# Output projection of three segments in half-row, half-column matmuls

## The chip, the cores and the metric

The kernel runs on one core of a Trainium2 chip. The metric is the device time of one execution in microseconds (us). The core has a matmul engine (PE, with a weight-load side PEld), a vector engine (DVE), a scalar engine (ACT), a general engine (POOL) and a queue that issues most transfers (SP). Each takes its instructions in the order written and waits on semaphores of the others.

## The reference, cut to what matters

```python
h = _layernorm(x) * (1 + ca) + sa
x = x + ga * _A_ref(h, wq, wk, wv, wo, beta)      # attention, 4 segments of 512 rows
h = _layernorm(x) * (1 + cb) + sb
x = x + gb * _B_ref(h, w1, b1, w2, b2)            # squared-ReLU feed-forward
...
# the end of _A_ref: o holds the four segments' heads, 2048 x 512
o = (...)(jnp.stack(outs, 2).reshape(B, H, S, Dh), 0, 2, 1, 3).reshape(B, S, D)
return o @ wo
```

S is 2048, D is 512, 32 heads of 16, four segments of 512 rows. The change concerns `o @ wo` of the first three segments, 1536 rows.

## The kernel before, in words

A row tile is 128 of the 2048 rows, so there are 16, numbered `g`, four to a segment. A product in single precision is made of three matmuls on values split in a high and a low part (`F32R`): high by high, high by low, low by high. `KD` is 4: the inner dimension of 512 is four chunks `k` of 128 (`P`).

`wo_tile(g)` handles the output projection of one row tile. SP loads the tile's attention output `ot` (from `o_dram`) and its input rows `xw`; PE turns `ot` round (four transposes into a PSUM bank, `bwot`, L1259); ACT casts that to the high part of `oT` (L1267), DVE subtracts to get the low part (L1269). Then PE runs, for each chunk, the three matmuls of `wo_mm` (L1233 to L1235, 128 rows by 512 columns) into one PSUM bank, `bwop`. DVE adds `xw` to that bank (L1276) and takes the row's statistics (L603, L604). `WVO` holds `wo`, multiplied by the gate row and split in parts: four loads (L1223), four DVE products (L1224), four ACT casts (L1225), four DVE subtractions (L1226). There are two `oT` buffers and eight PSUM banks.

The tiles of the first three segments are done while the fourth segment's attention runs; the matmuls of both are mixed on PE. Attention works in a different array form: `qk` and `vproj` (L795, L865), the score matmuls `ba` and `bpb` (L903, L1072), and the transposes `bfin` (L1166) use 64 of the array's 128 rows each, in pairs, one for the upper and one for the lower half. The products with V, `bpv` (L1131), use 32 columns each. So PE has three modes, called F (all rows), R (half the rows), C (32 columns).

`qk` and `vproj` already work by halves of the rows: in turn 0 the upper half writes bank 0 and the lower half bank 1, in turn 1 the other way round, and between the turns stands a `fence`: ACT copies one element of an operand onto itself (L771), after the last matmul of turn 0 and ahead of the first of turn 1.

Every step is a node of a `Plan` with its engine, duration, pools and predecessors. `ORDER` lists, for each engine, the numbers of the nodes in the order in which they are to be written out; where the list ends, a priority decides. The plan emits the nodes in that order, and the hardware keeps it.

Of the kernel before, what the change touches and what calls it, by code (L numbers as in the profile page):

```python
# [8 lines left out]
F32 = mybir.dt.float32  # L9
# [70 lines left out]
2146 496 1878-1880 1971 2128 2333 1974 2334 1978 2140 2335 2122 2336 1981 1882 2338 1986 2339 2143 2340 2131 2341 2259  # L80
2270 1990-1992 1994 2280 2001 2457-2458 2264 1997 2459 2152 2460 2009 2273 2004 2462-2463 2267 2238 2013 2246 2464
2159 2465 2162 2014-2015 2166 2243 498 2169 2017 2174 1968 2178 2249 2182 2179-2180 2276 2189 2185 2404 2192 2599 2252
2197 2201-2202 2255 2362 2203 2376 2367 2609 2602-2605 2283 2290 2612-2613 2298 2373 2286 2619 2614-2615 2293 2370
2205 2383 2622 2629 2623-2625 2632 2639 2302-2304 2306 2313 2397 2633-2635 2379 2321 2309 2486 2494 2642-2643 2316
2500 2644 2679 2645 2388 2407 2497 2325-2327 2391 2491 2682 2649 2683-2685 2414 2394 2417 2652-2653 2689 2654-2655
2400 2422 2329 2410 2507 2692 2728 2693 2720 2659 2694-2695 2430 2503 2426 2521 2437 2433 2427-2428 2445 2440 2518
2662 2732 2724 2663-2665 2699 2531 2515 2534 2449-2451 2512 2538 2702-2703 2524 2541 2453 2546 2704 2669 2705 2550
2554 2557 2561 2551-2552 2528 2564 2569 2672-2675 2709 2573-2575 2712 2577 2713-2715 2861 2863 2862 2777 2767 2864
2867 2866 2770-2771 2757 2865 2780 2772 2760 2773 2761 2787 2781 2762 2782-2783 2790-2792 2763 2885 2884 2886 2793
3024 2889 2887 3023 2888 3022 2890 3025 3027 2907 3104 2910 3026 2908 2912 2909 3028-3029 3092 2911 2913 3034  # L90
2930-2931 3032 3030 2936 2932 3040 3038 2933 3039 2934-2935 3036 2954 3042 2953 2956 3044 2955 3100 3041 3046 2959
2958 2957 3043 3047 3096 3050 2976 3045 2978 2977 3051 2981 3048-3049 2979 2982 3053 2980 2999 3057 3001 3000 3052
3005 3055 3054 3059 3002 3004 3061 3058 3056 3063 3132 3060 3064 3062 3003 3134 3067 3065 3135 3068 3136 3069 3072
3133 3073 3071 3066 3076 3159 3077 3137 3075 3084 3138 3081 3357 3070 3153-3154 3074 3155 3078 3157 3156 3158 3280
3349 3087 3174 3177 3175 3282 3279 3176 3361 3180 3286 3179 3178 3281 3195 3283 3285 3196-3197 3353 3199 3293 3198
3298 3291 3200 3287 3216 3201 3284 3217 3289 3219 3295 3218 3297 3302 3296 3221-3222 3300-3301 3306 3220 3299 3240
3304-3305 3237 3242 3239 3238 3310 3303 3309 3241 3308 3258 3261 3307 3314 3259 3243 3313 3312 3318 3260 3264 3311
3315-3316 3322 3262 3317 3263 3319 3390 3389 3618 3321 3393 3391 3326 3320 3610 3325 3323 3330 3392 3606 3324 3328
3327 3332 3395 3334 3394 3344 3329 3410 3333 3341 3411-3412 3414 3413 3331 3335 3338 3416 3415 3432 3436 3537-3538
3433 3431 3435 3536 3437 3539 3434 3540 3543 3452 3455 3454 3453 3542 3548 3544 3541 3457 3554 3550 3456 3474 3614  # L100
3546 3555 3552 3458 3556 3477 3558 3553 3473 3557 3560 3476 3475 3479 3559 3478 3564 3562 3495 3563 3566 3561 3565
3494 3496-3497 3499 3570 3569 3567 3573 3498 3516 3500 3515 3518 3577 3517 3574 3568 3571 3520 3572 3581 3519 3576
3575 3647 3521 3579 3578 3649 3580 3582 3584 3646 3583 3648 3585 3652 3586-3587 3651 3590 3650 3667 3588 3669 3668
3670 3591 3601 3592 3673 3589 3598 3595 3672 3671 3796 3691 3689 3688 3795 3800 3690 3693-3694 3799 3793 3692 3797
3794 3798 3709 3805 3711 3803 3801 3712 3710 3807 3713-3714 3810 3812 3809 3715 3731 3811 3730 3732 3736 3816 3820
3815 3814 3734 3733 3735 3819 3823 3754 3818 3813 3824 3751 3828 3753 3817 3822 3752 3827 3755-3756 3821 3825 3772
3757 3831 3826 3830 3776 3832 3829 3835 3774 3773 3775 3834 3777-3778 3836 3838 3840 3833 3839 3842 3844 3837 3841
3846 3852 3848 3858 3843 3847 3855 3845 3849
# [25 lines left out]
2109 240 2108 2113 2107 2111 2106 497 2112 2110 1881 1973 1972 1975-1976 1979-1980 2337 1983 1982 1987-1988 2133 2132  # L134
243 2342 2261 2348 2260 2344-2345 1993 1995 2002-2003 1996 1999 2153-2154 1998 2461 2011 2010 2006 2005 2239-2240 2161
2160 2164 2163 2016 2167-2168 499 2170-2171 2175-2176 2583 2184 2183 2181 2278 2277 2191 2190 2186-2187 2194 2193 2600
2595 2198-2199 2587 2591 2256-2257 2364 2363 2204 2466 2610 2472 2468-2469 2292 2291 2284-2285 2299-2300 2620 2288
2287 2295 2384 2294 2630 2385 2640 2314 2305 2315 2308 2307 2381 2380 2322 2311 2488 2323 2487 2317-2318 2310 2680
2408 2328 2650 2409 2415 2419 2416 2690 2418 2401-2402 2424 2423 2508 2411 2509 2729 2412 2721 2660 2505 2431 2504
2432 2438 2434 2439 2435 2429 2447 2441-2442 2446 2725 2733 2533 2747 2700 2536 2535 2532 2540 2452 2743 2526 2525  # L140
2543 2539 2547 2542 2749 2670 2548 2741 2556 2555 2559 2563 2562 2558 2739 2566 2751 2553 2745 2565 2571 2570 2710
2576 2868 2778 2768 2758 2799 2788 2876 2880 2877 2803 2878 2881-2882 2808 2891 2844 2899-2901 2903-2904 2914 3105
2812 3093 2905 2817 2922 2926 2923-2924 2937 2826 2927-2928 2821 2960 2945 2949 2835 2950 2830 2946 2951 2947 3101
2972 2968 2973-2974 2853 2983 3097 2848 2969 2857 2970 3115 3111 3006 2839 3113 2991-2992 3117 2995 3123 2993 2996
3014-3015 3121 2997 3016 3119 3018 3139 3019-3020 3358 3151 3160 3148 3350 3181 3169 3362 3172 3202 3354 3190 3223
# [20 lines left out]
1883-1884 2144-2145 2343 2272 2271 2349 2263 2281-2282 2265-2266 2275 2274 2269 2268 2247 2242 2248 2244-2245 2582  # L166
2018 1969 2019 2251 2250 2584 2594 2586 2590 2405-2406 2254 2253 2601 2596 2588 2592 2378 2369 2467 2611 2473 2377
2606 2368 2366 2374-2375 2621 2616 2372 2206-2207 2631 2371 2607 2387 2626 2641 2627 2399 2208 2398 2636 2617
2495-2496 2637 2502 2501 2681 2390 2499 2498 2646 2389 2392-2393 2492-2493 2651 2490 2395-2396 2686 2727 2691 2656
2723 2731 2719 2331 2330 2730 2722 2696 2661 2523 2522 2511 2519-2520 2687 2726 2734 2666 2517 2701 2516 2514 2513  # L170
2647 2697 2455 2657 2454 2706 2671 2750 2742 2332 2667 2456 2529 2744 2707 2530 2676 2711 2740 2677 2746 2578-2580
2716-2717 2748 2869 2752 2779 2769 2870 2872 2871 2874 2873 2759 2800 2875 2789 2774 2784 2804 2879 2883 2892-2893
2764 2895 2897 2894 2809 2794 3103 2896 2898 3352 2845 2795 3106 3095 3091 2813 2915 2902 2916 2918 2917 2920 3099
3094 2919 2921 2860 2906 2775 2827 3035 2938 2822 2939-2941 2925 2942-2943 2818 2944 2929 2961-2962 2964 2836 2831
# [3 lines left out]
3152 3166 3351 3079 3165 3167 3182 3168 3171 3088 3183 3363 3184-3185 3170 3187 3186 3188 3173 3203-3204 3355  # L178
3205-3206 3189 3208 3191 3207 3209-3210 3192 3224 3194 3225-3227 3294 3229 3212-3213 3228 3613 3605 3230-3231 3215
3245-3246 3233-3234 3247-3251 3266 3252 3236 3375 3609 3267-3268 3369 3269 3371 3254 3377 3270 3617 3272 3255 3802  # L180
# [216 lines left out]
def block_kernel(ctx, tc, x, wq, wk, wv, wo, beta, w1, b1, w2, b2, c, wmod, out):  # L397
# [842 lines left out]
    def wo_tile(g, pr):  # L1240
# [380 lines left out]
```

## Time and profile before

| what | value |
|---|---|
| time, median of 3 runs | 756.44 us (754.04 to 757.0) |
| the profiled execution, its own time | 754.31 us |
| its span, first to last instruction | 752.6 us |
| granted PE clock, share of full | 1.0 |
| PE busy | 739.3 us (98%), 6613 matmuls |
| DVE busy | 582.5 us (77%) |
| ACT busy | 431.4 us (57%) |
| POOL busy | 320.4 us (43%) |
| stretch of the 12 tiles | 358.4 to 436.2 us of the span |

The profile is of one execution. Busy is the time in which at least one instruction of the engine is in flight. A matmul's recorded duration is its latency, so what a matmul costs in a stream is read from the distance of two starts.

### The profile page before, as it was taken

What the parts mean: (1) busy time and instruction counts of PE and PEld (TensorE: products, weight loads), DVE (VectorE), ACT (ScalarE), POOL (GpSimd) and SP (SyncE); (2) the same over time, 40 slices, a digit from 0 to 9 for tenths busy, and PEclk for the clock granted to TensorE, in tenths of its full rate; (3) what the DMA queues carried; (4) which work ended last, traced back from release to release, by engine and by line L of the source; (5) the groups of instructions that cost most, each with busy time, mean ns of one, the idle gap of its engine ahead of it and who ended that gap; (6) DMA issues with size and microseconds to landing.
All of it is one profiled execution on the core that took longest, in us unless ns stands there. A gap on an engine that the chain in (4) does not pass through costs nothing.

```text
span 752.6 us, 17932 instructions
## 1 busy us (share of the span) xinstructions
PE 739.3 (98%) x6613; PEld 592.8 (79%) x6613; DVE 582.5 (77%) x1585; ACT 431.4 (57%) x959; POOL 320.4 (43%) x400
## 2 busy tenths in 40 slices
PE   8989999999999999999999999999999999999997
PEld 7876678666877677785666689998998899889986
DVE  6587888989899888898998967878865775576544
ACT  3668888899979987788667834553312312221110
POOL 5767758589968787364323532251020002000000
PEclk9999999999999999999999999999999999999999
DMA  9887763447544354457661067752644354437721
GB/s 302 247 234 237 236 193 91 132 135 198 167 135 133 93 136 142 104 139 232 189 204 58 2 224 264 267 211 99 212 180 161 134 201 191 170 137 280 272 92 57
DMA packets 61057, 129.65 MB, mean 172 GB/s; under 512 B 8613, under 2 KB 23977, under 8 KB 59178
## 3 DMA queue, kind: packets, MB, share of 16 engines
q1 hardware_dynamic: 60818, 128.37, 53.7%
q8 instruction: 53, 0.87, 0.5%
q14 instruction: 34, 0.28, 0.1%
q10 hardware_dynamic: 152, 0.13, 0.1%
HBM read 81.29 MB, written 20.19 MB: 135 GB/s over the span
## 4 chain that ended last, share of the span: by engine, by line
PE 85%; DMA 4%; ACT 3%; SPq 3%; POOL 2%; issue 1%; DVE 1%; ACTq 0%; POOLq 0%; DVEq 0%
PE bh L1501 18%; PE bqk L795 8%; PE bpv L1131 7%; PE bpf L1564 7%; PE bpf L1563 7%; PE bpf L1565 7%; PE bpb L1072 5%; PE bv L865 5%; PE ba L903 5%; PE bwop L1233 2%; SPq L844 2%; PE bwop L1235 2%; PE bwop L1234 2%; DMA ST<-sg 2%; PE bwarm L542 2%; DMA w1d<-X1L 1%
## 5 line engine op out<-in xcount | busy, mean ns | idle before, releaser
L908 DVE CUSTOM_DVE_ANT_0 ba<-ba,msk 128x384 f32<-128x384 f32 (+2 forms) x384 | 192.6, 532 | 26.7 <-PE ba L903 14.2
L1089 ACT ACTIVATE pt<-bpb 128x512 f32<-128x512 f32 x320 | 173.0, 619 | 19.0 <-PE bpb L1072 16.3
L1076 POOL TENSOR_SCALAR_AFFINE_SELECT pt<-pt 128x512 f32<-128x512 f32 x128 | 79.2, 638 | 75.2 <-ACT pt L1089 60.4
L795 PE MATMUL bqk<-HT,WQK 64*128 64x512 f32 x720 | 104.3, 397 | 0.2
L1131 PE MATMUL bpv<-pt,VT 128*32 128x512 f32 (+3 forms) x1024 | 81.1, 437 | 1.3 <-POOL pt L1076 0.4
L1072 PE MATMUL bpb<-ST 64*128 64x256 f32 (+2 forms) x512 | 78.5, 346 | 0.8 <-DMA ST<-mt 0.6
L903 PE MATMUL ba<-ST 63*128 63x256 f32 (+2 forms) x512 | 76.9, 343 | 2.3 <-DVE den L1003 1.1
L795 PEld LDWEIGHTS bqk<-HT,WQK 64*128 64x128 f32 x720 | 71.4, 185 | 9.3 <-ACT HT L771 1.3
L1072 PEld LDWEIGHTS bpb<-ST 64*128 64x128 f32 x512 | 51.0, 185 | 22.2 <-ACT pt L1089 5.2
L903 PEld LDWEIGHTS ba<-ST 63*128 63x128 f32 x512 | 51.2, 185 | 20.2 <-issue 5.2
L1545 ACT CAST ST<-xx 128x512 fp32r<-128x512 f32 x43 | 26.6, 620 | 69.4 <-DVE xx L1537 55.0
L1501 PE MATMUL bh<-ST 128*128 128x256 f32 x420 | 59.0, 282 | 0.0
L1501 PEld LDWEIGHTS bh<-ST,w 128*128 128x128 f32 x420 | 56.2, 190 | 3.4
L1501 PEld LDWEIGHTS bh<-ST 128*128 128x128 f32 x420 | 56.0, 189 | 3.1
L1501 PE MATMUL bh<-ST,w 128*128 128x256 f32 x420 | 58.3, 282 | 0.0
L865 PE MATMUL bv<-WVO,HT 64*128 64x512 f32 x384 | 57.4, 398 | 0.1
L1131 PEld LDWEIGHTS bpv<-pt,VT 128*32 128x32 f32 x1024 | 28.2, 109 | 34.3 <-issue 24.5
L908 DVE DVE_READ_ACCUMULATOR2_ANT mx<- 128x1 f32 x384 | 54.1, 141 | 0.0
L1332 POOL TENSOR_TENSOR tt<-h2raw 128x512 f32<-128x512 f32 x8 | 11.0, 1389 | 99.0 <-ACT h2raw L1297 77.7
L1563 PE MATMUL bpf<-w,ST 128*128 128x512 f32 x132 | 52.1, 395 | 0.0
L1564 PE MATMUL bpf<-w,ST 128*128 128x512 f32 x132 | 52.0, 394 | 0.0
L1565 PE MATMUL bpf<-w,ST 128*128 128x512 f32 x132 | 51.7, 391 | 0.0
(207 smaller groups left out, 1597.0 us busy)
## 6 DMA issues: line engine op xcount, KB each, us to landing
ST<-w1d SPq DMA_DIRECT2D x14, 1792.0 KB
w<-w1d SPq DMA_DIRECT2D x14, 1792.0 KB
ST<-sg SPq DMA_DIRECT2D x192, 128.0 KB
w1d<-X1L SPq DMA_DIRECT2D x21, 512.0 KB
xt<-in_A_x SPq DMA_DIRECT2D x16, 256.0 KB
wm<-in_w_mod SPq DMA_DIRECT2D x16, 256.0 KB
xw<-in_A_x SPq DMA_DIRECT2D x16, 256.0 KB
X1L<-in_B_w SPq DMA_DIRECT2D x7, 512.0 KB
```

What stands on the lines that cost most here:

```text
L795: nc.tensor.matmul(bank(banks[w]), W3(w, k, x, cols.start, cols.stop)[r], HT[r, y, k], start=first and i == 0, stop=last and i == 2)
L865: nc.tensor.matmul(bank(banks[t]), HT[r, x, k, (t2 + t) * P:(t2 + t + 1) * P], WVO[r, k, y], start=first and i == 0, stop=last and i == 2)
L903: nc.tensor.matmul(dst[:, c0:c0 + n], ST[b:b + 63, 0, sl, qt * P:(qt + 1) * P], ST[b:b + 63, 1, sl, :n], start=True, stop=True)
L908: nc.vector.tensor_tensor_reduce(i, i, msk[:, 512 - n:], scale=1.0, scalar=-3e38, op0=ALU.add, op1=ALU.max, accum_out=o)
L1072: nc.tensor.matmul(dst, ST[b:b + 64, 1, sl, kb * P:(kb + 1) * P], ST[b:b + 64, 0, sl, q0:512], start=True, stop=True)
L1076: nc.gpsimd.affine_select(out=ap, in_=ap, pattern=[[0, ap.shape[1]], [1, P]], compare_op=ALU.is_ge, fill=0.0, base=0, channel_multiplier=-1)
L1089: ns = [op("ACT", 0.49, lambda j=j: nc.scalar.activation(buf("PPP"[n], pt)[:, i + j], bank(keys[j]), AF.Exp, scale=0.25), pr[slot] + 0.01 ...
L1131: nc.tensor.matmul(bank(o)[32 * hq:32 * hq + 32, q0:q0 + src.shape[1]], v[:, a:a + 32], src, start=start, stop=stop, tile_position=(0, 32 ...
L1501: nc.tensor.matmul(pb(i), A[:, x, kk], B[:, y, kk], start=kk == j == 0, stop=kk == 1 and j == 2)
L1563: nc.tensor.matmul(q, rh, wh, start=(i == 0), stop=False)
L1564: nc.tensor.matmul(q, rh, wl, start=False, stop=False)
L1565: nc.tensor.matmul(q, rl, wh, start=False, stop=(i == NF - 1))
```

## The change

For the twelve tiles of the first three segments, `wo_tile` no longer calls `wo_mm`. The product is made in the half-row form of `qk`: two PSUM banks, one for each half of the 512 columns; in turn 0 the upper 64 rows of a chunk make the left columns and the lower 64 the right, in turn 1 the other way round. A tile is 48 matmuls of 64 rows by 256 columns in place of 12 of 128 rows by 512, and a fence on ACT stands between its turns. DVE adds `xw` in two pieces of 256 columns. The last segment's four tiles stay as they were. `ORDER` is drawn anew from a point in the last segment's `qk` on.

```diff
-2146 496 1878-1880 1971 2128 2333 1974 2334 1978 2140 2335 2122 2336 1981 1882 2338 1986 2339 2143 2340 2131 2341 2259
+2146 496 1878-1880 1971 2128 2333 1974 2334 1978 2140 2335 2122 2336 1981 1882 2338-2339 1986 2143 2340 2131 2341 2259
...
         n = None
-        for k in range(KD):
-            n = pe("F", 0.699, lambda k=k: wo_mm(bank(b2), TL[ot], k), pr + 0.03 + 0.002 * k,
-                   after=[n] if k else [h, l, *WON], get=() if k else [("#D", b2)], put=[ot] if k == KD - 1 else ())
-        WOL.append(n)
-        n = dve(512, lambda: nc.vector.tensor_tensor(x1(g), bank(b2), TL[xk], op=ALU.add), pr + 0.05, after=[n, ld], put=[b2, xk])
+        if last:
...
+        else:
+            bs_ = [("wop", g, c) for c in (0, 1)]
+
+            def mm(turn, k, i):
+                for q, (x, y) in enumerate(((0, 0), (0, 1), (1, 0)) if turn else ((0, 1), (1, 0), (0, 0))):
+                    for j in (1, 0) if turn else (0, 1):
+                        c, r = j ^ turn, slice(64 * j, 64 * j + 64)
+                        nc.tensor.matmul(bank(bs_[c])[:, :256], TL[ot][r, x, k * P:(k + 1) * P], WVO[r, k, y, 256 * c:256 * c + 256],
+                                         start=turn == i == q == 0, stop=turn == 1 and i == KD - 1 and q == 2)
+            for turn in (0, 1):
+                for i in range(KD):
+                    k = KD - 1 - i if turn else i
+                    if turn and not i:
+                        n = op("ACT", 0.2, lambda k=k: nc.scalar.copy(TL[ot][64:65, 0, k * P:k * P + 1],
+                                                                      TL[ot].bitcast(F32)[64:65, 0, k * P:k * P + 1]), pr + 0.035, after=[n])
+                    n = pe("R", 0.36, lambda turn=turn, k=k, i=i: mm(turn, k, i), pr + 0.03 + 0.002 * (4 * turn + i),
+                           after=[n] if n else [h, l, *WON], get=() if turn or i else [("#D", q) for q in bs_],
+                           put=[ot] if turn and i == KD - 1 else ())
+            WOL.append(n)
+            n = [dve(256, lambda c=c: nc.vector.tensor_tensor(x1(g)[:, 256 * c:256 * c + 256], bank(bs_[c])[:, :256],
+                                                              TL[xk][:, 256 * c:256 * c + 256], op=ALU.add),
+                     pr + 0.05, after=[n, ld], put=[bs_[c], xk]) for c in (0, 1)]
+            n[0].outs.append(n[1])
+            n[1].left += 1
+            n = n[1]
```

In the changed kernel's listing, lines up to the tile are two higher than before (L1072 is L1074, L903 is L905); the new matmuls are L1287, the fence L1293, the half adds L1299.

On PE, at the first tile of the stretch, before (`bwop` is the projection, `bpb` are scores):

```order
L1233 MATMUL bwop<-WVO,oT 128x512
L1234 MATMUL bwop<-WVO,oT 128x512
L1235 MATMUL bwop<-WVO,oT 128x512
L1072 MATMUL bpb<-ST 128x512 x2
L1072 MATMUL bpb<-ST 128x256 x2
L1072 MATMUL bpb<-ST 128x384 x2
L1233 MATMUL bwop<-WVO,oT 128x512
L1234 MATMUL bwop<-WVO,oT 128x512
L1235 MATMUL bwop<-WVO,oT 128x512
```

and on PE at the first tile now (`ba` are scores too, `bfin` transposes by halves):

```order
L905 MATMUL ba_6599<-ST 128x512
L905 MATMUL ba_6600<-ST 128x512
L1287 MATMUL bwop<-WVO,oT 128x256 x18
L905 MATMUL ba_6633<-ST 128x512
L905 MATMUL ba_6634<-ST 128x512
L1287 MATMUL bwop<-WVO,oT 128x256 x6
L1168 MATMUL bfin<-ident,oraw 128x64 x16
L1287 MATMUL bwop<-WVO,oT 128x256 x12
L1074 MATMUL bpb<-ST 128x512 x2
L1287 MATMUL bwop<-WVO,oT 128x256 x12
```

The first 24 are turn 0, the last 24 turn 1; all rows of this piece are in mode R, where before the projection's rows in mode F alternated with rows in mode R. Over the whole program PE changes mode 159 times before and 144 times now.

On ACT at the same place, with the first two fences (`CAST oT<-oT`; `pt` are the exponentials), now:

```order
L938 COPY ac<-ba_6563 128x512
L938 COPY ac<-ba_6564 128x512
L1157 COPY oraw<-bpv 128x512
L837 ACTIVATE phi_6622<-bqk 128x512
L1293 CAST oT<-oT 1x1
L835 ACTIVATE e<-bqk 128x512
L1091 ACTIVATE pt<-bpb 128x512 x4
L1269 CAST oT<-bwot 128x512
L1091 ACTIVATE pt<-bpb 128x512 x2
L1293 CAST oT<-oT 1x1
```

The fences stand among copies and exponentials of 512 columns; twelve of them are new and nothing of the rest is gone.

On DVE ahead of the first tile, where `wo` is made ready (`den` is the memory read's denominator), before:

```order
L1226 TENSOR_TENSOR WVO<-wo,WVO 128x512
L1224 TENSOR_TENSOR wo<-wo,gab 128x512 x3
L1003 SCALAR_TENSOR_TENSOR den<-bmr,ge 128x16
L1005 RECIPROCAL den<-den 128x16
L1006 TENSOR_TENSOR am<-bmr,den 128x4x64
```

and on DVE there now:

```order
L1226 TENSOR_TENSOR wo<-wo,gab 128x512
L1050 TENSOR_TENSOR tm<-bmu,bdm 128x34
L1226 TENSOR_TENSOR wo<-wo,gab 128x512 x2
L910 ISA ba_6456,mx<-ba_6456,msk 128x384
```

The products with the gate row now stand ahead of the score maxima (`ba`), and `den` comes ten rows later. On SP the four `wo` loads stood between other loads of the tile, now all four are issued before the first `ot` load.

More of the change, by code (lines that the diff above doesn't have):

```diff
@@ L150 @@
+3090 3211 3091-3092 3430 3223 3232 3220 3422 3253 3241 3434 3244 3274 3426 3262 3295 3283 3265 3286 3304 3316 3442
[3 rows of a table added]
 """,
@@ L1271, in wo_tile @@
         n = None
-        for k in range(KD):
-            n = pe("F", 0.699, lambda k=k: wo_mm(bank(b2), TL[ot], k), pr + 0.03 + 0.002 * k,
-                   after=[n] if k else [h, l, *WON], get=() if k else [("#D", b2)], put=[ot] if k == KD - 1 else ())
-        WOL.append(n)
-        n = dve(512, lambda: nc.vector.tensor_tensor(x1(g), bank(b2), TL[xk], op=ALU.add), pr + 0.05, after=[n, ld], put=[b2, xk])
+        if last:
+            for k in range(KD):
+                n = pe("F", 0.699, lambda k=k: wo_mm(bank(b2), TL[ot], k), pr + 0.03 + 0.002 * k,
+                       after=[n] if k else [h, l, *WON], get=() if k else [("#D", b2)], put=[ot] if k == KD - 1 else ())
+            WOL.append(n)
+            n = dve(512, lambda: nc.vector.tensor_tensor(x1(g), bank(b2), TL[xk], op=ALU.add), pr + 0.05, after=[n, ld], put=[b2, xk])
+        else:
[15 more added lines that the diff above has]
+                           put=[ot] if turn and i == KD - 1 else ())
+            WOL.append(n)
+            n = [dve(256, lambda c=c: nc.vector.tensor_tensor(x1(g)[:, 256 * c:256 * c + 256], bank(bs_[c])[:, :256],
[4 more added lines that the diff above has]
+            n = n[1]
```

146 lines of the change are left out of this document (74 added, 72 removed), and 13 rows, old and new, of the table ORDER.

## The prediction

> **What bounds the kernel now.** I read the page's engine sums and the shares of its chain first, then the stretch in which the twelve tiles run, then who waits on PE there.
>
> ```profile
> PE 739.3 (98%) x6613; PEld 592.8 (79%) x6613; DVE 582.5 (77%) x1585; ACT 431.4 (57%) x959; POOL 320.4 (43%) x400
> PE 85%; DMA 4%; ACT 3%; SPq 3%; POOL 2%; issue 1%; DVE 1%; ACTq 0%; POOLq 0%; DVEq 0%
> 358.40:436.17 77.77, 77.75 (x646) 53.05 (x643) 71.45 (x199) 53.82 (x113) 28.11 (x40) 1.00 0.40 120
> ```
>
> PE carries the chain. The third line is the stretch from the score matmuls just before the first projection to the last tile's end: 77.77 us, PE busy 77.75, then PEld, DVE 71.45 (92%), ACT 53.82 (69%), POOL, the granted clock (1.00) and the share of the transfers. PE does not pause there, so what the change adds to or takes from PE's stream moves the end, as long as no other engine makes PE wait. From 330 to 440 us one wait of PE is listed:
>
> ```profile
> PE ba L903 <- DVE den L1003: 1.1, 1, 1.1
> 352.08 1.29 DVE L1224 TENSOR_TENSOR wo<-wo,gab 128x512 f32<-128x512 f32 x2 [0.85 <-DMA wo<-in_A_wo]
> 353.29 0.17 DVE L1003 SCALAR_TENSOR_TENSOR den<-bmr,ge 128x16 f32<-128x16 f32 x1
> 346.81 0.34 SPq L1223 DMA_DIRECT2D wo<-in_A_wo  x1
> ```
>
> DVE stood still 0.85 us until a `wo` load had landed, did two products, and only then `den`; PE waited 1.1 us for that. It is just ahead of the stretch.
>
> **The change, part by part.** First, what a mode change costs. PE at the first tile, and two places in mode R alone:
>
> ```profile
> 359.90 0.39 PE L1234 MATMUL bwop<-WVO,oT 128*128 128x512 f32 x1
> ...
> 362.23 0.40 PE L1235 MATMUL bwop<-WVO,oT 128*128 128x512 f32 x1
> 362.56 0.79 PE L1072 MATMUL bpb<-ST 64*128 64x512 f32 x6
> 363.28 0.51 PE L1233 MATMUL bwop<-WVO,oT 128*128 128x512 f32 x1
> 363.62 0.39 PE L1234 MATMUL bwop<-WVO,oT 128*128 128x512 f32 x1
> 83.50 0.68 PE L795 MATMUL bqk<-HT,WQK 64*128 64x512 f32 x4
> 83.97 0.45 PE L1072 MATMUL bpb<-ST 64*128 64x256 f32 x4
> 84.21 0.67 PE L795 MATMUL bqk<-HT,WQK 64*128 64x512 f32 x4
> 157.00 0.70 PE L903 MATMUL ba<-ST 63*128 63x256 f32 x8
> 157.53 0.64 PE L795 MATMUL bqk<-HT,WQK 64*128 64x512 f32 x4
> ```
>
> From 359.90 to 362.23 are ten full matmuls in a row: 0.233 each. From 83.50 to 83.97 are two pairs of 512 columns: 0.235 a pair. From 83.97 to 84.21 are two pairs of 256: 0.12 a pair. From 157.00 to 157.53 are, by the code, three pairs of 256 and one of 384: 0.53 less 0.36 leaves 0.17 for the pair of 384. The six score matmuls at 362.56 are one pair of each width, so 0.235 + 0.12 + 0.17 = 0.525. From 362.23 to 363.62 are two full matmuls (0.466), these six, and two changes of mode: 1.39 - 0.466 - 0.525 = 0.40, so **0.20 us a change**.
>
> Removed: the order has 159 changes of mode before and 144 now, 15 fewer, at 0.20: **-3.0 us**. All lie on PE's stream.
>
> Replaced: 12 x 12 = 144 full matmuls at 0.233 are 33.55 us; 12 x 24 = 288 pairs at 0.12 are 34.56 us. **+1.0 us**, on PE too. The transposes of `ot` stay in mode F and keep their changes, which the count includes.
>
> Here a rule speaks against the change. The Trainium skill, TensorE: Matmul & The Clock Gate, Part 2, LDWEIGHTS, says that a weight load takes its number of columns divided by 1.2 GHz, however few rows it fills; a tile now loads 48 times 128 columns instead of 12 times. Taken one after another, two loads a pair would be 213 ns, an estimate from that page, and the sum would be about +28 us. The pairs of 256 columns at 83.97 also load 128 columns for each of their four matmuls and still pass at 0.12, so the trace is against it, in runs of up to three pairs only; the rival below has it with prices from rows.
>
> Added: twelve fences. What one costs is seen where little stands between its turns:
>
> ```profile
> 112.26 0.55 PE L903 MATMUL ba<-ST 63*128 63x512 f32 x2
> 112.51 0.55 PE L1072 MATMUL bpb<-ST 64*128 64x512 f32 x2
> 112.86 0.72 PE L865 MATMUL bv<-WVO,HT 64*128 64x512 f32 x3
> 112.61 0.19 ACT L771 CAST WVO<-WVO 1x1 fp32r<-1x1 f32 x1 [0.24 <-PE bv L865]
> L771 ACT CAST HT<-HT x15: 187/187/189, 27.4 to 335.8; 1x1 fp32r<-1x1 f32 x15
> L771 ACT CAST WVO<-WVO x8: 187/188/188, 34.9 to 311.3; 1x1 fp32r<-1x1 f32 x8
> PEld bqk L795: 1.3, 2
> PEld bv L865: 0.2, 1
> 418.38 0.49 PE bfin L1166 x16
> L1089 ACT ACTIVATE pt<-bpb 128x512 f32<-128x512 f32 x320 | 173.0, 619 | 19.0 <-PE bpb L1072 16.3
> ```
>
> Turn 0 ended before 112.26, ACT was free and ran the fence at 112.61, turn 1 began at 112.86. Between stood two pairs of 512, 0.47 us of work, that took 0.60: PE lost 0.13. Of the 23 fences of before PE's weight side waited after three, 1.5 us together, 0.065 a fence. The new ones have at the first tile 16 `bfin` matmuls between the turns, 0.49 us by the row at 418.38, about what stood at 112.26; by the order four of twelve tiles have so little, the rest more. If a fence also sits behind an exponential that has just begun, it is up to 0.62 later (L1089's mean). So the bounds are 0 and 12 x (0.13 + 0.62) = 9.0 us; I take the nearest row, 12 x 0.065: **+0.8 us**. Behind a fence on ACT queue exponentials that PE's V products wait for; at 0.19 each, twelve are 2.3 us in a stretch where ACT has 24 us free, so nothing for that.
>
> Split: DVE's add of 512 columns becomes two of 256.
>
> ```profile
> L1276 DVE TENSOR_TENSOR X<-bwop,xw 128x512 f32<-128x512 f32 x11 | 7.6, 687 | 0.7 <-PE bwop L1235 0.4
> L1183 DVE TENSOR_TENSOR X1L<-bfin,dn 128x256 f32<-128x256 f32 x8 | 3.4, 424 | 0.3
> 387.00:395.00 8.00, 8.00 (x65) 5.49 (x58) 7.93 (x24) 3.23 (x6) 0.51 (x1) 1.00 0.53 190
> ```
>
> 24 x 0.424 - 12 x 0.687 = +1.9 us of DVE work. What hides it is that PE is longer: 77.8 - 1.2 = 76.6 us against 71.45 + 1.9 = 73.4. That is 96%, and in 387 to 395 DVE was already busy 7.93 of 8. If the cover is gone it costs up to 1.9. I take 0, since PE did not pause even in that piece. Two PSUM banks instead of one are held by a tile until DVE has added; of that no row of before shows a price, and I count it in the same bound.
>
> Moved: the `wo` loads go ahead of the first `ot` and `xw` on SP, behind more of the `ST` fills, and on DVE the products go ahead of the score maxima. The load issued at 346.81 landed 5.27 us later, at 352.08. Issued before `ot`, it could land earlier and the 1.1 us wait go; or DVE, which now reaches the products earlier, stands longer with the maxima behind it, on which PE waits for banks. Bounds -1.1 and, as the nearest row of a wait at this place, +1.1. I take 0. The rest of the order after the stretch feeds the feed-forward part with the same work, at nothing: PE has no pause there to lose or gain.
>
> Sum: -3.0 + 1.0 + 0.8 = **-1.2 us**. Against the profiled execution's own 754.31 that is 753.1. The runs shown are 754.04, 756.44 and 757.0, so that execution was 2.1 below their median; the four lie about 755.4, and I put the time at 754.2.
>
> **The rivals.** *The fences and DVE eat the gain.* Place: between turn 0 and turn 1, where a fence waits behind a running exponential. Half of 0.62 for the wait and 0.13 for the trip are 0.44 each, 5.3 in all in place of 0.8: -2.0 + 5.3 = +3.3, so about 758.7. It turns to a loss from 2.0 us in all, 0.17 a fence. For it: ACT is 69% busy, and DVE is as full as said. Against: 20 of 23 fences before cost nothing, on an ACT that was then busier.
>
> *The wait for `wo` goes as well.* -1.2 - 1.1 = -2.3, and -3.1 if the fences are free too: 752.3 to 753.1. For it: all four loads before `ot`. Against: twelve fills are put before or between them.
>
> *Weight loads bound the pairs.* This one ends far on the slow side.
>
> ```profile
> 408.88 0.87 PE blnq L616 x8
> ```
>
> These are full transposes, each with a load of 128 columns and as many streamed, 0.109 each. If in a long run of pairs each half's load took that and went after the other, a pair would be 0.218, a tile 5.2 instead of 2.8, twelve +29, so near 782. It decides from a pair of 0.124 on, where the sum is zero with 288 pairs; 0.5% slower is at 0.138. For it: before the change, no run of 256-column pairs is longer than three. Against: 0.12 at all places above. TensorEngine Tiling (Array Packing) of the Trainium skill, Key Properties, says that different tiles can load and multiply in parallel; the trace's 0.12 agrees.
>
> *The change does not do what it says.* If the 0.40 were not the modes but, say, the first weights of a group, the fewer changes save nothing: +1.0 + 0.8, so 757.2. Against: at 83.97 a change of line, tile and width without a change of mode costs nothing.
>
> **How the numbers follow.** The forecast's case has 0.55, the wait going too 0.2, fences and DVE 0.17, no saving 0.05, weight loads 0.03. The range: low is the lowest run with the gains and no fence cost, 754.0 - 3.0 + 1.0 - 1.1 = 751; high is the median with DVE and the wait at their upper bounds, 756.4 - 1.2 + 1.9 + 1.1 = 758.2, and 758.5 to take in most of the first rival. About what a measurement of this kernel tells from no change is 0.5%, 3.8 us. Beyond that to the fast side lie the wait's case at its end with some luck elsewhere, 0.14; to the slow side the weight loads and the worst fences, 0.07; the rest, 0.79, is within.
>
> **What would show it.** PE's stretch of the twelve tiles about 2 us shorter with no pause; pairs of L1287 at 0.12 from start to start; after each fence L1293 less than 0.15 us until turn 1; DVE at 95% or more of the stretch; `den` not waited for. The prediction is wrong if PE's weight side waits for L1293 by more than 2 us in all, if DVE's adds (L1299) appear as what PE waits for, or if pairs pass slower than 0.124.

## The result, and the profile after

The changed kernel takes 750.82 us (median of 6 runs, 749.99 to 752.62) against 755.02 for the kernel before on the same chip: ratio 0.9942, 95% interval 0.9924 to 0.9961. On another chip, with 12 runs, it was 752.21 against 754.37: 0.9967, 0.9952 to 0.9983. So it is faster, by 0.3 to 0.6%; the prediction said 754.2, in a range that began at 751.0.

The profiled execution has an own time of 750.63 us and a span of 748.9. These are the engine sums and the shares of the chain:

```profile
PE 736.3 (98%) x7045; PEld 602.8 (80%) x7045; DVE 585.4 (78%) x1597; ACT 433.4 (58%) x971; POOL 320.9 (43%) x400
PE 77%; DMA 6%; POOL 4%; ACT 4%; issue 3%; SPq 3%; DVE 2%; POOLq 0%; ACTq 0%
```

PE has 432 matmuls more and is busy 3.0 us less. Its waits between 320 and 440 us, by the list of waits:

```profile
PE bpb L1074 <- DVE mx L910: 0.2, 1, 0.2
PE bpb L1074 <- ACT mt L972: 0.2, 1, 0.2
```

The 1.1 us wait for `den` is not there. Before, three of the four `wo` loads were issued ahead of the first `ot` and the fourth behind that tile's `ot` and `xw`; now, by the timeline, the last two are issued together ahead of the first `ot`. DVE makes the last two products without a listed wait, and `den` comes later than before, behind score maxima and subtractions:

```profile
345.59 1.09 SPq L1225 DMA_DIRECT2D wo<-in_A_wo  x2
347.10 0.33 SPq L1250 DMA_DIRECT2D ot<-o_dram  x1
348.96 1.41 DVE L1226 TENSOR_TENSOR wo<-wo,gab 128x512 f32<-128x512 f32 x2
353.87 0.17 DVE L1005 SCALAR_TENSOR_TENSOR den<-bmr,ge 128x16 f32<-128x16 f32 x1
```

Over all profiles of this study, the time from the start to the last matmul of the gate row (`bmodr`, L582, in the changed kernel L584) lies between 343.9 and 348.7 us, also where nothing ahead of it was altered (in the profile with 348.7 PE was granted half its clock for 10.2 us ahead of it). So spans of single profiles don't tell the change's worth. I compare two stretches behind it: **A**, from that matmul to the first projection matmul, and **B**, from there to the first feed-forward matmul (`bh`). What follows, to the end of the last matmul, takes 312.7 to 313.0 us in all but two of them (313.5 and 314.0), before and after. Here are the two stretches by windows of the trace, with the columns of the prediction's third line: first of the kernel before,

```profile
344.40:359.50 15.10, 13.87 (x181) 8.13 (x180) 13.09 (x39) 13.45 (x31) 5.88 (x8) 1.00 0.58 186
359.50:436.00 76.50, 76.47 (x633) 52.10 (x632) 70.18 (x197) 52.72 (x111) 28.11 (x40) 1.00 0.41 122
```

and then of the changed kernel:

```profile
344.20:357.80 13.60, 13.08 (x176) 7.52 (x176) 13.21 (x37) 13.45 (x32) 5.54 (x8) 1.00 0.76 235
357.80:432.20 74.40, 74.40 (x1069) 61.66 (x1067) 69.30 (x207) 55.17 (x121) 27.86 (x40) 1.00 0.39 118
```

A is 1.5 us shorter in this pair of profiles and B 2.15. PE does not pause in B in either kernel, and DVE has 5 us to spare (69.30 of 74.40, 93%).

All runs, with A and B from the starts of the matmuls in each trace. The mode changes are counted up to the one into `bh`. The third column is the time that DVE stood idle ahead of the four products of `wo` with the gate row. The medians come from several chips, and each ratio given below is against the kernel before on the same chip:

| kernel | A, us | DVE idle ahead of the `wo` products, us | B, us | mode changes in B | median time, us |
|---|---|---|---|---|---|
| before, three profiles | 15.11, 14.88, 14.71 | 1.53, 1.37, 1.24 | 76.45, 76.46, 76.48 | 42 | 755.02; 755.07; 755.17 |
| changed, two profiles | 13.61, 13.48 | 0.04, 0 | 74.30, 74.26 | 27 | 750.82; 752.21 |
| old order, last two `wo` loads early, two profiles | 14.47, 15.21 | 1.10, 1.48 | 76.44, 76.43 | 42 | 755.02; 754.47 |
| changed, one `wo` load behind the loads of two tiles | 17.73 | 3.44 | 74.63 | 27 | 757.41 |
| changed, one `wo` load behind those of one tile | 18.06 | 3.67 | 75.05 | 27 | 757.19 |
| new order, full tiling | 13.58 | 0 | 85.39 | 92 | 762.81 |
| old order, half rows | 14.48 | 0.94 | 87.86 | 39 | 767.49 |
| changed, fences threefold | 13.48 | 0 | 76.97 | 27 | 754.03 |
| changed, order drawn again | 14.44 | 0.59 | 74.68 | 27 | 752.83 |
| three transposes by halves too | 13.12 | 0 | 74.18 | 21 | 751.37 |

### The profile page after: what moved, and what is told of

Its sections match the earlier page's. It is cut to its first block, busy times and chain, and to the rows that moved or that the text cites. A ratio compares the mean times of both kernels' runs of the same rounds, so it can differ in the third digit from the quotient of the medians.

```text
span 748.9 us, 18830 instructions
## 1 busy us (share of the span) xinstructions
PE 736.3 (98%) x7045; PEld 602.8 (80%) x7045; DVE 585.4 (78%) x1597; ACT 433.4 (58%) x971; POOL 320.9 (43%) x400
## 4 chain that ended last, share of the span: by engine, by line
PE 77%; DMA 6%; POOL 4%; ACT 4%; issue 3%; SPq 3%; DVE 2%; POOLq 0%; ACTq 0%
PE bh L1529 19%; PE bpv L1133 7%; PE bpf L1592 7%; PE bpf L1591 7%; PE bpf L1593 7%; PE bqk L797 6%; PE bpb L1074 5%; PE bwop L1287 5%; PE ba L905 4%; PE bv L867 4%; DMA w1d<-X1L 2%; SPq L846 2%; ACT pt L1091 1%; PE bwot L1261 1%; POOL WQK L711 1%
## 5 line engine op out<-in xcount | busy, mean ns | idle before, releaser
L1133 PE MATMUL bpv<-pt,VT 128*32 128x128 f32 (+3 forms) x1024 | 81.1, 437 | 1.1 <-ACT pt L1091 0.4
L1074 PE MATMUL bpb<-ST 64*128 64x256 f32 (+2 forms) x512 | 79.1, 344 | 1.4 <-ACT pt L1091 0.4
L905 PE MATMUL ba<-ST 63*128 63x256 f32 (+2 forms) x512 | 76.4, 340 | 2.0 <-DMA ST<-sg 1.3
L1074 PEld LDWEIGHTS bpb<-ST 64*128 64x128 f32 x512 | 51.5, 185 | 20.8 <-ACT pt L1091 4.3
L905 PEld LDWEIGHTS ba<-ST 63*128 63x128 f32 x512 | 51.0, 185 | 18.5 <-issue 4.9
```

Source lines behind the costliest of these rows:

```text
L905: nc.tensor.matmul(dst[:, c0:c0 + n], ST[b:b + 63, 0, sl, qt * P:(qt + 1) * P], ST[b:b + 63, 1, sl, :n], start=True, stop=True)
L1074: nc.tensor.matmul(dst, ST[b:b + 64, 1, sl, kb * P:(kb + 1) * P], ST[b:b + 64, 0, sl, q0:512], start=True, stop=True)
L1133: nc.tensor.matmul(bank(o)[32 * hq:32 * hq + 32, q0:q0 + src.shape[1]], v[:, a:a + 32], src, start=start, stop=stop, tile_position=(0, 32 ...
```

## The experiments

**Form and order apart.** The change makes the product in another form and draws the order anew. First the new order with the old form: the nodes of the changed kernel's order, each full chunk in the place of two half-row chunks.

```diff
-    (twelve tiles: 48 matmuls of 64 rows by 256 columns, fence, two adds)
+    (twelve tiles: 12 matmuls of 128 rows by 512 columns, one add, as before)
     ORDER: that of the changed kernel on every engine
```

> The changed kernel's order on every engine, but each of the twelve tiles made with the full tiling of before (12 matmuls of 128 rows by 512 columns, no fence, one add); each full chunk stands where two half-row chunks stood. PE then changes mode 210 times, against 144 in the changed kernel and 159 before. Theory (0.20 us a change, 0.233 a full matmul, 0.12 a pair): 66 x 0.20 - 1.0 = +12.2 us against the changed kernel, so about 763, nearly all of it in the projection's stretch, 74.3 -> about 86.5; per change 0.18 to 0.22. Rival (the changes cost little here, or are hidden because DVE and ACT set the pace of the stretch): +1 to +6.

B by windows:

```profile
361.50:447.00 85.50, 85.50 (x637) 50.90 (x636) 70.94 (x196) 52.84 (x110) 28.37 (x40) 1.00 0.36 103
```

762.81 us, ratio 1.01 (1.0047 to 1.0154); B is 85.39 against 74.30. All of it is PE's: busy throughout, with fewer matmuls. The work is 0.43 us less than in the changed kernel (144 x 0.233 = 33.55 against 288 pairs at the 0.118 that they take there, 33.98), so the 65 changes of mode that B has more, 92 against 27, cost 11.09 + 0.43 = 11.52 us, **0.177 each**. Against the kernel before, whose matmuls in B are the same but for two pairs of scores (0.29 us), B has 50 changes more and is 8.93 us longer: 0.173 each. The theory's price of 0.20 stands, a little lower. The Trainium skill, TensorEngine Tiling (Array Packing), Key Properties, says that a change of tiling mode drains the engine; the trace agrees, with 0.177 us a change. A is 13.58, as short as in the changed kernel: what was gained there belongs to the order and not to the half-row form.

Then the old order with the new form.

```diff
+    (twelve tiles in the half-row form with their fences, as in the changed kernel)
     ORDER: that of before on every engine; w0 w1 fence w2 w3 -> two half-row chunks for each w
```

> The changed kernel's half-row form of the twelve tiles, but in the order of before on every engine: two half-row chunks stand where one full chunk stood, both half adds where the add stood, and each fence where ACT comes to it in that order. PE changes mode 157 times (159 before, 144 in the changed kernel), and in seven of the twelve tiles turn 1 follows turn 0 with nothing between them on PE. Theory (the form gains nothing by itself: the gain is fewer changes, which need the new order, and a fence is free only where about 0.6 us of other work stands between the turns): against before's 76.45 us from the first projection matmul to the first feed-forward matmul, +1.1 for the pairs, -0.4 for two changes, 7 x 0.57 + 0.3 for bare fences = +5.0, so 81 to 82, up to 84 where a fence sits behind a long ACT instruction; ahead of the first projection as before (15.1 us from the last gate matmul, L584, within 0.5). Rival 1 (the form itself gains, by weight loads of 64 rows running beside the other half): 74 to 75.5. Rival 2 (PE has slack in its queue and a bare fence costs under 0.2): 76.5 to 78.

B by windows:

```profile
361.00:448.90 87.90, 82.15 (x1063) 62.96 (x1062) 71.99 (x208) 55.73 (x122) 28.13 (x40) 1.00 0.37 110
```

The first tile on the timeline, where turn 1 follows turn 0 on PE with nothing between, and its fence on ACT:

```profile
362.06 1.46 PE L1287 MATMUL bwop<-WVO,oT 64*128 64x256 f32 x21
363.80 0.98 PE L1287 MATMUL bwop<-WVO,oT 64*128 64x256 f32 x12 [0.28 <-ACT oT L1293]
363.56 0.19 ACT L1293 CAST oT<-oT 1x1 fp32r<-1x1 f32 x1 [1.26 <-PE bwop L1287]
```

767.49 us, ratio 1.016 (1.0127 to 1.0193). The 21 matmuls from 362.06 on are 1.26 us of work at 0.06, and turn 1 begins 1.74 after them: a bare fence costs PE 0.48. In the seven tiles where it is bare the starts show 0.49 to 0.74, 4.0 us together, which is what was expected. But B grew by 11.4, not by 5 to 8: PE is busy only 82.15 of 87.90 us, since scores and V products wait for other engines too. I did not follow those waits one by one, so the rest of the 11.4 stays open. That the form alone gains is refuted, at any rate: in the old order it loses, and in its own order B without the form is 11 us longer than with it.

**The fences.** In the changed kernel, the group of the fences and that of the half adds:

```profile
L1293 ACT CAST oT<-oT 1x1 fp32r<-1x1 f32 x12 | 2.2, 187 | 4.9 <-PE bwop L1287 4.7
L1299 DVE TENSOR_TENSOR X<-bwop,xw 128x256 f32<-128x256 f32 x24 | 9.5, 416 | 0.8 <-PE bwop L1287 0.8
```

and the first tile's turns on the timeline of PE (turn 0 ends with the first row, turn 1 begins with the third):

```profile
359.15 0.52 PE L1287 MATMUL bwop<-WVO,oT 64*128 64x256 f32 x6
359.51 0.66 PE L1168 MATMUL bfin<-ident,oraw 64*128 64x64 f32 x16
360.01 0.97 PE L1287 MATMUL bwop<-WVO,oT 64*128 64x256 f32 x12
```

Between the turns stand the 16 `bfin`, 0.49 us of work by the prediction's row, and they took 0.50. ACT stood idle 4.7 us, six times, for turn 0 to end: the fence waited, PE did not. Is that because the cover is ample, or just enough? I made each fence longer.

```diff
-                        n = op("ACT", 0.2, lambda k=k: nc.scalar.copy(TL[ot][64:65, 0, k * P:k * P + 1], ...), ...)
+                        n = op("ACT", 0.6, lambda k=k: [nc.scalar.copy(TL[ot][64:65, 0, k * P:k * P + 1], ...) for _ in range(3)], ...)
```

> The changed kernel with each of its twelve fences made three times over on ACT (three copies of one element in place of one), 0.37 us more on ACT between the turns. By the trace of the changed kernel four fences end 0.05 us before the first load of turn 1 starts (tiles whose cover is 0.5 us of other work), four end 0.13 to 0.28 before it, the rest more than 0.5. Theory (the cover is just as long as the trip at the tightest tiles, so that the fence is free with nothing to spare): 4 x 0.37 + 4 x about 0.17 = +1.5 to +2.2 us in the projection's stretch. Rival 1 (PE is held by something else at these places, and the cover is ample): within 0.4 us. Rival 2 (ACT's order is the tight thing and each fence delays exponentials that PE needs): 12 x 0.37 = +4.4 or more.

The view of the fence's line, its group and who waited for it (us in total, times):

```profile
L1293 ACT CAST oT<-oT x36: 187/187/188, 361.7 to 434.8; 1x1 fp32r<-1x1 f32 x36
PEld bwop L1287: 2.3, 6
PE bwop L1287: 0.9, 4
```

754.03 us, ratio 0.9981 (0.9965 to 0.9997); B is 76.97 against 74.30, 2.7 more, of 12 x 0.37 = 4.5 us put on ACT. From the last matmul's start of turn 0 to the first of turn 1 it is now 0.99 to 1.05 us in eight tiles, with 0.57 to 0.90 in the same tiles of the changed kernel; the differences add up to 2.2. A bare fence, in the run above, was 0.55 to 0.56 by the same measure where ACT was free. So the trip of a single fence is as long as the work that the order leaves at its four tightest tiles (0.57 to 0.62): free with nothing to spare. The measured 2.7 lies a little above the theory's 1.5 to 2.2; where the other 0.5 of it went is not shown. Neither rival fits, the one with 0.4 at most or the one with 4.4.

**The `wo` loads.** On SP, `2581`, `2585`, `2589` and `2593` are the four `wo` loads, `2598` the first tile's `ot` and `xw`, `2614` the second's (`2608` in the old order). The old order with the last two loads early:

```diff
-... 2353 2581 2593 2359 2589 2598 2585 2355 2608 ...
+... 2353 2581 2593 2589 2585 2359 2598 2355 2608 ...
```

> The kernel before, full tiling and its old order, with one thing moved: on SP the last two wo loads go ahead of the first row tile's ot and xw loads, as in the changed kernel. Theory (the changed kernel gained 2.15 us by fewer mode changes in the projection and 1.5 us because DVE no longer stood waiting for wo ahead of it): the 0.85 us wait of DVE's wo product and the 1.1 us wait of PE for den go, the first projection matmul comes 0.8 to 1.5 us earlier than 359.56, the time is 0.8 to 1.5 us below before's. Rival 1 (the 1.5 us came from the rest of the new order on PE and DVE, not from the loads): the waits move to another load or to the first ot, first projection within 0.3 us of 359.56, time the same. Rival 2 (first ot, now issued behind 0.5 MB more, is late): the first projection comes 0.5 us or more later. All three expect the projection's stretch itself to stay at 76.4 us.

755.02 us, ratio 0.9997 (0.9974 to 1.002). A was 14.47 in place of 15.11, which looked like half of the theory's gain. But the half-row form in the old order, whose loads had not moved, also showed 14.48 and no wait for the fourth load. So I profiled both orders again:

> The kernel before, unaltered, profiled again. In its first profile DVE waited 0.85 us for the fourth wo load and the first projection came 15.11 us after the last gate matmul; in the run of the half-row form in the old order, whose loads stand in the same places, DVE did not wait for it and it was 14.48. Theory A (the wait belongs to the old order): 15.1 within 0.2, with a wait for wo of 0.7 to 1 us. Theory B (the load lands just about when DVE comes to it, some tenths earlier or later from run to run, so the wait is there in some executions only): 14.4 to 15.2, and where it is near 14.5 no wait for wo is listed. Both: the projection's stretch 76.4 within 0.2.

> The kernel before, unaltered, a third profile, for the same question: theory A 15.1 within 0.2, theory B 14.4 to 15.2, stretch 76.4 within 0.2.

> The old order with all four wo loads ahead of the first ot, once more. It gave 14.47 us ahead of the projection, without a wait for wo. Both theories expect 14.5 within 0.2 again; by theory B that is also what the kernel before gives in the executions in which its fourth load lands in time, so that moving the loads is worth 0 to 0.65 us, not 0.65 each time.

They took 755.07 us (ratio 1.0, 0.998 to 1.002), 755.17 (0.9998, 0.9974 to 1.0022) and 754.47 (1.0005, 0.9985 to 1.0025). From the lists of waits between 345 and 362 us, of the kernel before in its second profile:

```profile
DVE wo L1224 <- ACT pt L1089: 1.2, 1, 1.2
DVE wo L1224 <- DMA wo<-in_A_wo: 0.2, 1, 0.2
PE ba L903 <- DVE tm L1048: 0.5, 1, 0.5
PE ba L903 <- DVE den L1003: 0.4, 1, 0.4
```

of the same kernel in its third:

```profile
DVE wo L1224 <- ACT gab L584: 0.6, 1, 0.6
DVE wo L1224 <- DMA wo<-in_A_wo: 0.6, 1, 0.6
PE ba L903 <- DVE den L1003: 0.8, 1, 0.8
```

and of the old order with the last two loads early, second profile:

```profile
DVE wo L1224 <- ACT pt L1089: 1.5, 1, 1.5
PE ba L903 <- DVE tm L1048: 1.1, 1, 1.1
```

DVE's wait for the fourth load was 0.85, 0.17 and 0.59 us in three profiles of one kernel. With the last two loads early it is gone, and A is 14.90 on average of three with them late and 14.84 of two with them early: no gain that these five profiles show, where they differ among themselves by 0.7. The theory gave this 0.8 to 1.5 us, and it falls.

But that does not say that the loads are worth nothing. DVE makes four products, and it stood at the first one too. In the first profile of before, and in the first with two loads early:

```profile
346.11 0.69 DVE L1224 TENSOR_TENSOR wo<-wo,gab 128x512 f32<-128x512 f32 x1 [0.68 <-ACT gab L584]
349.51 0.69 DVE L1224 TENSOR_TENSOR wo<-wo,gab 128x512 f32<-128x512 f32 x1 [1.10 <-ACT pt L1089]
```

In the lists above it is the line of 1.2, of 0.6 and of 1.5 us. The exponential `pt` is no operand of this product, and `gab`, the gate row, was ready 0.4 to 1.2 us before the product started in these five profiles. In the second profile of before the trace has the last part of the first `wo` load landing 0.08 us before the product starts, so there the wait ended with that load. The experiment left the first load at its place in the order, issued 1.75 to 2.14 us ahead of the gate matmul (344.45 in the first profile of before). In the changed kernel (344.26) it is issued 3.52 us ahead, and the first product starts as soon as the gate row is ready. The first load's issue, before and changed:

```profile
342.37 1.82 SPq L1223 DMA_DIRECT2D wo<-in_A_wo  x2
340.73 0.60 SPq L1225 DMA_DIRECT2D wo<-in_A_wo  x1
```

All waits at the four products together are 1.24 to 1.53 us before and 1.10 to 1.48 with two loads early: the sum did not fall, which is what rival 1 says. Over the six profiles of the old order A rises with this sum, from 14.5 where it is 0.94 and 1.10 to 15.1 and 15.2 where it is 1.53 and 1.48, and in the four of the new order without a load put back both are smallest. Whether the first load's earlier place does it alone is not shown: no run moved that load and nothing else.

In the changed kernel the place of a single load matters. I put one of the last two back, once behind the first tile's loads and once behind the first two tiles'.

```diff
-... 2593 2350 2351 2585 2589 2598 2614 ...
+... 2593 2350 2351 2589 2598 2585 2614 ...   (one tile)
+... 2593 2350 2351 2589 2598 2614 2585 ...   (two tiles)
```

> The changed kernel with the last-consumed-but-one wo load (k = 1 of four) put back behind the first two row tiles' ot and xw loads on SP; nothing else is changed. Theory: DVE's product on that load waits again, with den queued behind it, so PE waits again and the first projection matmul comes 0.5 to 2 us later than 357.87, the time is 0.5 to 2 us above the changed kernel's; the projection's stretch stays at 74.3 us. Rival 1 (the loads' place is not what gained): first projection within 0.3 us of 357.87, time the same.

> The changed kernel with one wo load (k = 1) put back behind the first row tile's ot and xw loads only, which is its place in the kernel before; in the run where it stood behind the loads of two tiles, DVE waited 2.95 us for it and the first projection came 17.7 us after the last gate matmul instead of 13.6. Theory (each load put ahead of it on SP delays its landing by about its own 0.5 us of issue and a share of the transfer, and DVE, PE behind it, waits for that): the load is issued about 1.2 us later than in the changed kernel and lands 1 to 2.5 us later; DVE waits 0.5 to 2 us, the first projection comes 14.1 to 15.6 us after the last gate matmul, the stretch behind it stays at 74.3 within 0.4. Rival (what delayed the other run was two tiles' loads of 1 MB on the wire, one tile's load is hidden): 13.6 within 0.3.

757.41 us, ratio 1.0038 (1.0014 to 1.0062), and 757.19, ratio 1.003 (1.001 to 1.005). Both lengthen A by more than 4 us, against 0.5 to 2 expected. In the run with one tile, on the timeline, the load on SP, DVE waiting for it, and PE's wait:

```profile
349.22 0.42 SPq L1225 DMA_DIRECT2D wo<-in_A_wo  x1
354.49 1.69 DVE L1226 TENSOR_TENSOR wo<-wo,gab 128x512 f32<-128x512 f32 x2 [2.91 <-DMA wo<-in_A_wo]
356.78 1.27 PE L998 MATMUL bmr<-MB,phi 64*128 64x68 f32 x14 [2.00 <-ACT pt L1091]
```

and then windows of a microsecond, in which the granted clock is the third number from the end:

```profile
357.00:358.00 1.00, 1.00 (x17) 0.91 (x17) 0.97 (x7) 1.00 (x3) 0.00 (x0) 1.00 0.81 297
358.00:359.00 1.00, 1.00 (x11) 0.87 (x10) 1.00 (x3) 0.65 (x2) 0.68 (x2) 0.79 0.43 164
359.00:360.00 1.00, 1.00 (x7) 1.00 (x5) 1.00 (x2) 0.56 (x2) 1.00 (x1) 0.50 0.00 0
360.00:361.00 1.00, 1.00 (x6) 0.20 (x8) 0.93 (x4) 1.00 (x3) 0.22 (x1) 0.50 0.00 0
361.00:362.00 1.00, 1.00 (x8) 0.00 (x0) 0.93 (x4) 0.69 (x2) 0.42 (x1) 0.50 0.45 82
362.00:363.00 1.00, 1.00 (x18) 0.52 (x18) 1.00 (x3) 0.23 (x3) 0.00 (x0) 1.00 0.78 299
```

The load was issued 2.89 us after the gate matmul, against 1.33 in the changed kernel, and the product that waited for it began 5.27 later. PE stood 2.00 us; the releaser named is an exponential, and I did not trace the steps between it and DVE. Then something came that no theory had: from 358.6 to 362.0 PE was granted half its clock. 3.4 us at half clock are 1.7 us of work lost, so the 4.45 us are 2.0 of waiting, 1.7 of slow clock and 0.75 of smaller things.

**Looking for more.** The changed kernel with the order of the same stretch drawn once more, nothing else altered, the changed kernel itself beside it, and a version in which three tiles' transposes of `ot` are made by halves too:

```diff
-ORDER (from the last segment's qk to the end of the twelve tiles)
+ORDER (drawn again; on SP: 2585 2357 2581 2589 2354 2593 2598 2614 ...)
```

> The changed kernel with nothing altered but the order, drawn once more for the same stretch: on PE the transposes of three more tiles stand next to a block of another mode (142 changes against 144), the fences of the tightest tiles have 0.1 to 0.3 us more between their turns, on SP all four wo loads go ahead of the last ST fills and of the first ot, and on DVE the four products stand a little earlier among the maxima. Theory (what is left in the changed kernel are changes at 0.2 us and about 1.3 us of stall ahead of the first projection): 2 x 0.2 = 0.4 us less in the projection's stretch plus 0 to 0.3 at the fences, 0.3 to 1 us less ahead of it; 0.7 to 1.7 us faster than the changed kernel, about 4.5 to 5 us faster than before. Rival (the order found for the changed kernel is as good as the chip allows, since the new one is drawn by durations that are not exact): within 0.5 us of the changed kernel, to either side.

> The changed kernel unaltered, on the same chip as the other two, for the comparison. All theories: 13.6 us from the last gate matmul to the first projection matmul and 74.3 from there to the first feed-forward matmul, within 0.2; 3.5 us faster than before within the measurement.

```diff
+            for k in range(KD):
+                for j in (0, 1):
+                    w = slice(64 * j, 64 * j + 64)
+                    nc.tensor.transpose(bank(bb[j])[:, 64 * k:64 * k + 64], TL[o][w, k * P:(k + 1) * P], ident[w, w])
```

> The changed kernel, and besides the ot transposes of three tiles (2, 4 and 9, which stood alone between stretches of mode R) made by halves of the rows too: eight transposes of 64 by 128 into two PSUM banks in place of four of 128 by 128 into one, ACT's cast and DVE's subtraction in two pieces of 256 columns; the order drawn again for it. Theory (a change costs 0.2): about 6 changes fewer than the changed kernel in the projection's stretch, 1.2 us, and 3 x 0.19 = 0.6 for the transposes themselves (eight at 0.031 in place of four at 0.109), against a second bank held per tile and 3 x 0.16 more on DVE and up to 1 us of new waits for banks: stretch 72.5 to 73.8 against 74.3. Rival (PSUM banks are the tight thing: tiles that hold two for the transposes and two for the product keep the scores waiting): stretch 74.5 to 77.

The redrawn order by windows, A and then B:

```profile
346.10:360.60 14.50, 13.56 (x178) 7.63 (x178) 13.57 (x38) 13.71 (x32) 5.01 (x7) 1.00 0.63 190
360.60:435.30 74.70, 74.47 (x1069) 61.35 (x1066) 69.33 (x206) 54.80 (x121) 29.34 (x42) 1.00 0.40 125
```

and PE's waits in it between 340 and 455 us:

```profile
PE bpb L1074 <- DVE mx L910: 0.4, 1, 0.4
PE bpb L1074 <- DVE tm L1050: 0.4, 1, 0.4
PE bpb L1074 <- DMA ST<-mt: 0.2, 1, 0.2
```

It took 752.83 us, ratio 0.9974 (0.996 to 0.9987), beside 0.9967 (0.9952 to 0.9983) for the changed kernel on the same chip: no better, against 0.7 to 1.7 us expected. B has as many changes as in the changed kernel (the two that went lie in A), and A is almost a microsecond longer: DVE again stands 0.27 and 0.32 us at the first two `wo` products, and PE's two waits of 0.4 us lie there. The third, of 0.2 for a fill of `ST`, lies in B. The transposes by halves took 751.37, ratio 0.9964 (0.9947 to 0.998), the same as the changed kernel. By their trace B has 6 changes and 0.57 us of transposes less, 1.6 us together at 0.177, and B is 74.18, 0.1 less; the trace shows 0.42 us of idle PE in B, and where the rest went is not shown. A is 0.4 us shorter, but what follows B took 314.0 us, 1.1 more than in the changed kernel. Of the three, none beats the changed kernel by what can be measured.

## Why the prediction was right or wrong

- **The mode changes: right.** Predicted 15 fewer at 0.20, -3.0. B has 15 fewer, and the new order with full tiles puts a change at 0.177, so -2.7. The rival that the changes save nothing is refuted by that run.
- **Pairs at 0.12: right**, and with it the end of the weight-load rival. The longest runs of the half-row matmuls in the changed kernel:

```profile
389.36 1.97 PE L1287 MATMUL bwop<-WVO,oT 64*128 64x256 f32 x30
391.14 0.42 PE L905 MATMUL ba<-ST 63*128 63x512 f32 x2
395.56 1.57 PE L1287 MATMUL bwop<-WVO,oT 64*128 64x256 f32 x24
396.98 0.45 PE L1074 MATMUL bpb<-ST 64*128 64x256 f32 x4
```

  1.78 us for 15 pairs and 1.42 for 12: 0.119 and 0.118 a pair, also in runs five times longer than any of before; taken one after another, the two halves' weight loads would have made it 0.218 by the prediction's own row. 288 pairs at 0.118 against 33.55 are +0.4, not +1.0.
- **The fences: mechanism right, size wrong.** +0.8 was an average over 23 old fences, the price at the row at 112.26 being 0.13. Measured: one listed wait of 0.2 us, and nothing at the first tile. From the last matmul's start of turn 0 to the first of turn 1 the row at 112.26 has 0.67 us, behind a matmul of 512 columns; a bare fence here has 0.56, behind one of 256. The work that stands between is about the same, 0.47 and 0.49, so little of the 0.13 is left: 0.50 us for 0.49 of work at the first tile. The rival that the fences and DVE eat the gain needed 0.17 a fence. It did not come, but a fence 0.37 us longer would have brought it.
- **DVE's split adds: right** that they are hidden. 24 x 0.416 is 10.0 us; DVE is at 93% of B, not at the predicted 95 or more.
- **What is moved: this is the term that failed.** It was taken as 0 with bounds of 1.1 to both sides. A is 13.54 us in the four profiles with the new order and no load put back (changed twice, full tiling, threefold fences) and 14.81 in the six with the old (before three times, loads early twice, half rows): -1.27. Of that, 0.53 us are score matmuls that left A, no gain: two pairs (0.29) now stand behind the first projection, one (0.24) ahead of the gate matmul. The other 0.74 is stall that is gone. The prediction read one wait of DVE, the one for the fourth `wo` load, and set its chance to go against as much harm. It did not read the wait of 0.68 us at the first product, nor that the first load is issued 3.52 us ahead of the gate matmul in place of 2.08. Moving the last two loads alone gained nothing; in the new order DVE's waits at the four products, 0.94 to 1.53 us in the old, are 0.04 at most, and PE's stall went with them (by the windows PE stood 1.23 us in A before and 0.52 now). How much of the 0.74 is the first load's place and how much the order on DVE and PE stays open.
- **The sum.** From the gate matmul to the first feed-forward matmul: before 91.36 us (mean of three), changed 87.83 (of two), -3.5; 0.24 of it only went ahead of the gate matmul, so -3.3. Terms: changes -15 x 0.177 = -2.7, pairs +0.4, stall -0.74: -3.0. The other 0.3 is open; it would be nothing if the changes that went were worth the prediction's 0.20, and no run prices them by their kinds. The forecast's -1.2 was short by the fences' 0.8, by 0.6 on the pairs and by the stall. The rival *the wait for `wo` goes as well*, with free fences at -3.1, named the size and what came: DVE no longer stands at the `wo` products. Its reason, all four loads ahead of the first `ot`, did not suffice, as the two runs with early loads show.
- **The range** began at 751.0, the lowest run with the gains. The first comparison lies 0.2 under it, the second inside, and 755.0 less the traces' 3.3 is 751.7, inside too: that the first fell out is chance in part. That the forecast has a third of the gain is not. It left out that the new order could be better by more than the one wait that it listed.

## What to carry to other kernels

Where PE is the bound and works in several array forms, count the changes of form in the order and price them from two rows of the trace; a form that streams no faster can still win if it lets neighbours stay in one form; here it did so only with the order drawn for it. A hop to another engine and back is free if the work put between is as long as the trip, so compare these two lengths and not the engine's load. And when the profile lists one wait on an engine that is late, do not book that wait as the gain or as nothing: add up that engine's waits for the same thing, in more than one profile, and see whether a change ends them or passes them on.

## What the runs showed of the hardware

- A change between the array forms costs PE 0.17 to 0.18 us: 0.177 from 65 changes against the changed kernel, 0.173 from 50 against the kernel before.
- PE to ACT and back, through a copy of one element of 0.187 us, is 0.56 us from the last matmul's start to the next one's where the matmuls have 256 columns, and 0.67 at the row at 112.26 where they have 512; with three copies and 256 columns it is 1.00.
- In the two runs with a `wo` load put back PE stood for 2.0 us, ran on at full clock for 1.8 us (one tile) and 1.1 us (two tiles), and then had 0.50 of it for 3.4 us. The length of the pause alone does not decide it: in the new order with full tiling a pause of 2.3 us at 86.6 us was followed by no half clock, while in the second profile of before and in the redrawn order pauses of 1.4 and 1.0 us at 47.3 and 47.4 us were followed by 3.4 us of it at 50.7 and 50.6 us. What decides it stays open. The Trainium skill, TensorE: Matmul & The Clock Gate, Part 1, says that the clock halves after an idle window of about 3.4 us, and warns against pauses above about that; here pauses of 2.0 us and less were followed by it. The length of the slow spell, 3.4 us, agrees with the window it states.
- A `wo` load of 256 KB was followed 5.27 us after its issue by the product that waited for it, where other loads were under way, and DVE's wait for it varied from 0.17 to 0.85 us between profiles of one program.
